# Experts' second product of one token group with the weights standing and 384 tokens moving

## The chip, the core and the metric

The kernel runs on one core of one Trainium2 chip. A core has TensorE (PE, matmuls), VectorE (DVE), ScalarE (ACT), GpSimd (POOL) and SyncE (SP, which here only issues DMAs), each with its own instruction queue, and 16 DMA engines that they share. The metric is the device time of one execution in microseconds; three runs of the kernel before gave a median of 1117.77 (1117.68 to 1119.88).

## The reference

Everything is float32. Attention without softmax, a bilinear layer, and a mixture of four experts follow one another:

```python
kv  = einsum('bhsd,bhse->bhde', k, v)            # 4 x 8 heads, 576 tokens, 64 wide
out = einsum('bhsd,bhde->bhse', q, kv)
x   = out / sqrt(mean(out**2) + 1e-6) * g_norm   # -> [2304 tokens, 512]
x   = ((x @ w1) * (x @ w2) @ w3) @ w_out         # 1024 wide inside
p   = domain_probs / (domain_probs.sum(-1) + 1e-9)
for e in range(4):                               # the experts
    y += p[:, e] * (relu(x @ e_w1[e]) @ e_w2[e]) # 512 -> 1024 -> 512
```

The change touches the experts' second product, `relu(...) @ e_w2[e]`, its scaling by the token's share `p[:, e]`, the sum over the experts, and the store of the result.

## The kernel before

A float32 value is held as two parts, high and low, and a product is three matmuls (high x high, low x high, high x low), by the helper `mm3` (L321 to L325); so nearly all of TensorE's time stands under L323 to L325. Larger products are cut in two each way and done by a seven-product scheme (Winograd's form of Strassen) in place of eight.

The 2304 tokens go through the experts in three groups of 2 x 384 tokens (`GROUPS`, `W = 384`; a part of a group is three tiles of 128 tokens). The first group computes the second product plainly (`down`) and spills the weights and their sums to DRAM (`w2_kept`). The second and the third group use `up` for the first product, with weight tiles of 128x128 standing and 384 tokens moving, and `down_product` (L1523) for the second. One call of `down_product` is one of the seven products of one expert (`PRODUCTS`, L1480): it loads the w2 operand in two DMAs of 512 KB into buffers of a pool of five (`RAWS`, L1531 to L1538), makes the token operand and splits it into high and low (`tokens_operand`, L1491, with sums at L1501 and splits at L368 and L373), and then, for each of the three token tiles, lets the tokens stand (128x128) and 256 columns of w2 move: 4 pieces x 3 passes (L1545 to L1550). The sums of the seven products collect in four PSUM banks, two (`at`) by two; a product that ends a target or feeds one is read out by `collect_half` (L1564), which multiplies by the share, a number per token and so per partition, and adds to the tile's accumulator in one VectorE operation (L1576); the first one of a tile is a ScalarE or VectorE operation that writes it (L1580, L1582). When the last expert has been added, `store_tile` (L1616) stores the 128 tokens x 512 on SyncE's queue in one DMA.

The order of all work is written by a planner (`Plan.order`, L139). Each operation has durations for the engines that may do it, a stage (its place in the list of items built at L1648 to L1677), and buffers. The planner runs a list schedule with these durations: an engine that is free takes the ready operation of the earliest stage, up to 14 stages ahead (`WINDOW`), if its buffers fit (99 SBUF tiles of 2 KB a partition, 8 PSUM banks), so matmuls of the second product fill the places where the first product waits for its bank. On the chip each engine then runs its list in that order, waiting on semaphores. VectorE's operations between SBUF tiles and GpSimd's are marked as sharing one port (`ported`, L116) and are not planned at the same time. The items of one expert's second product stand among those of the next expert's first product; at a change of group three products (`AHEAD`) stand before it. The shares `pn` are computed once in the front part (`expert_shares`, L1637).

Of the kernel before, what the change touches and what calls it, by code (L numbers as in the profile page):

```python
# [9 lines left out]
F32 = mybir.dt.float32  # L10
# [5 lines left out]
ALU = mybir.AluOpType  # L16
AX = mybir.AxisListType

P = 128
# [4 lines left out]
WINDOW = 14  # L24
AHEAD = 3
LATER = 6
PLAIN = 1
SUMMING = 18
WARM = 10
# [66 lines left out]
class Plan:  # L96
# [11 lines left out]
    def add(self, engines, emit, reads=(), writes=(), latency=0.2, stage=None, free=False, hold=None):  # L108

        op = Op(engines, emit, self.stage if stage is None else stage, latency)
        op.hold = hold
        op.ported = {e for e in engines if e == "pool" or (e == "dve" and not free)}  # L116
        op.pinned = stage is not None
        for accesses, write in ((reads, False), (writes, True)):
            for access in accesses:
                buf, key = access if isinstance(access, tuple) else (access, None)  # L120
                if buf not in op.bufs:
                    op.bufs.append(buf)
                    buf.users += 1
                for other, k, w in buf.touched:
                    if other is not op and (write or w) and (k is None or key is None or k == key):
                        op.deps.append(other)
                buf.touched.append((op, key, write))
        op.index = len(self.ops)
        self.ops.append(op)
        return op  # L130
# [128 lines left out]
def attention_moe_kernel(  # L259
# [26 lines left out]
    nc = tc.nc  # L286
    B, H, S, D = q.shape
    NT, DM = out.shape
    FF = moe_w1.shape[1]
    NE = e_w1.shape[0]  # L290
    HP = H // 2
    KD = DM // P
    KF = FF // P
    R = 4
    M = R * P
# [12 lines left out]
    plan = Plan({"r": RAWS, "h": TILES, "n": 4, "c": 2, "b": BANKS, "d": 1000, **RINGS})  # L308
    add = plan.add
# [4 lines left out]
    def bank():  # L314
        return Buf("b", "b", [P, 512], F32)

    def half(name, dt=F32, ring=None):
        return Buf("h", name, [P, 512], dt, ring)


    def mm3(ps, w, x, first, last, more=False):  # L321

        nc.tensor.matmul(ps, w[0], x[0], start=first, stop=False, skip_group_check=more)  # L323
        nc.tensor.matmul(ps, w[0], x[1], start=False, stop=False, skip_group_check=more)  # L324
        nc.tensor.matmul(ps, w[1], x[0], start=False, stop=last, skip_group_check=more)  # L325

    def t_act(n, psum=False):
        return (0.157 if psum else 0.19) + n / 1200

    def t_dve(n):  # L330
        return 0.143 + n / 960
# [4 lines left out]
    def t_pe(n, passes=3):  # L336
        return passes * (0.0137 + n / 2400)
# [16 lines left out]
    def spilled(name, buf, value=whole, later=0):  # L354

        d = Buf("d", name, [P, 512], F32, tag=name)
        add(
            {"sp": 0.73}, lambda _: nc.sync.dma_start(out=d[:, :], in_=value(buf.tile)),
            reads=[buf], writes=[d], latency=2.4, stage=plan.stage + later,
        )  # L360
        return d
# [41 lines left out]
    ident = const.tile([P, P], F32, name="ident")  # L403
    g8 = const.tile([P, 1], F32, name="g8")
    pn = const.tile([P, NT // P, NE], F32, name="pn")
# [4 lines left out]
    xscale, share = Buf("c", "xscale", None, None), Buf("c", "share", None, None)  # L410
# [258 lines left out]
    def evacuate(dst, src, n, to, value, key=None):  # L669
        add(  # L670
            {"act": t_act(n, True), "dve": t_dve(n)},
            lambda e: nc.scalar.copy(to(dst.tile), value(src.tile)) if e == "act"  # L672
            else nc.vector.tensor_copy(out=to(dst.tile), in_=value(src.tile)),
            reads=[src], writes=[(dst, key)], free=True,
        )
# [191 lines left out]
    def pair_weights(g, n, i):  # L867
# [3 lines left out]
        f0, f1 = i, i + KF // 2  # L871
        if g and i < PLAIN:
            raw = Buf("r", "wval", [P, 2, 512], F32)
# [12 lines left out]
        else:  # L886
            vals = [weight(n, f) for f in (f0, f1)]
            if i < PLAIN:
                w12_kept[n, i] = [
                    spilled(f"w{n}kept{i}_{j}", val, later=LATER) for j, val in enumerate(vals)  # L890
                ]
                made = pair_w[g, n, i] = {}, [Pair("w"), Pair("w")]
                for val, w in zip(vals, made[1]):
# [4 lines left out]
                [  # L898
                    spilled(f"w{n}_{i}_{m}_{part}", t, lambda t: t.bitcast(F32), later=LATER)
                    for part, t in enumerate(pair.parts)  # L900
# [6 lines left out]
    def weight(n, f):  # L907

        if (n, f) not in weights:
            weights[n, f] = decode(f"w{n + 1}", columns((moe_w1, moe_w2)[n], f), True)  # L910
        return weights[n, f]

    def bilinear_plain(b, i):

        ws = [pair_weights(0, n, i)[1] for n in range(2)]
        for j, f in enumerate((i, i + KF // 2)):
            multiplied(b, f, [w[j] for w in ws])
            ab[b, f] = spilled(f"ab{b}kept{f}", ab[b, f], later=LATER)

    def bilinear_pair(g, i):  # L920
# [77 lines left out]
        for b in (b0, b1):  # L998
            for f in (f0, f1):
                ab[b, f] = spilled(f"ab{b}kept{f}", ab[b, f], later=LATER)  # L1000

# [130 lines left out]
    W = 384  # L1132
    TILES3 = W // P
# [12 lines left out]
    def token_tile(g, i, t):  # L1146
        whole_block, half_block, at = GROUPS[g]
        return (whole_block, 2 * i + t) if t < 2 else (half_block, at // P + i)
# [342 lines left out]
    def tokens_operand(g, e, name, i):  # L1491

        a = {
            f"a{part + 1}{k + 1}": h32[g, e, i + k * KF // 2, part] for part in range(2) for k in range(2)
        }

        def sum_of(name, x, y, op):
            t = sums[g, e, name, i] = half(name)
            add(
                {"dve": t_dve(W)},  # L1500
                lambda eng: nc.vector.tensor_tensor(  # L1501
                    out=t[:, :W], in0=x[:, :W], in1=y[:, :W], op=op
                ),
                reads=[x, y], writes=[t],
            )
            return t

        def get(name):
            if name in a:
                return a[name]  # L1510
            if (g, e, name, i) in sums:
                return sums[g, e, name, i]
            x, y, op = {
                "s1": ("a21", "a22", ALU.add), "s2": ("s1", "a11", ALU.subtract),
                "s3": ("a11", "a21", ALU.subtract), "s4": ("a12", "s2", ALU.subtract),
            }[name]
            return sum_of(name, get(x), get(y), op)

        s = Pair("ht")
        split(s, get(name), W, lambda t: t[:, :W], lambda t: t[:, :W])  # L1520
        return s

    def down_product(g, e, n):  # L1523
        left, right, at, start, targets = PRODUCTS[n]
        if n == 0:
            yacc[g, e] = [[bank(), bank()] for _ in range(2)]
        banks = yacc[g, e][at]
        k = W2_OPERANDS.index(right)
        kept = w2_kept[e]
        lefts, rights = [], []  # L1530
        for i0 in range(0, KF // 2, 2):  # L1531
            raw = Buf("r", "w2", [P, 2, 2, 256], F32R)
            add(
                {"sp": 1.46},
                lambda _, raw=raw, i0=i0: nc.sync.dma_start(out=raw.tile.bitcast(F32), in_=kept.tile[:, k, i0:i0 + 2]),
                reads=[kept], writes=[raw], latency=2.4,
            )
            rights += [(raw, 0), (raw, 1)]  # L1538
        for i in range(KF // 2):
            lefts.append(tokens_operand(g, e, left, i))  # L1540
        for t in range(TILES3):
            ps = banks[t // 2]
            c = slice(t % 2 * 256, t % 2 * 256 + 256)

            def mms(_, t=t, ps=ps, c=c):  # L1545
                for i, (h, (raw, r)) in enumerate(zip(lefts, rights)):
                    mm3(
                        ps[:, c], h[:, t * P:(t + 1) * P], (raw[:, r, 0], raw[:, r, 1]),
                        start and i == 0 and t % 2 == 0, i == KF // 2 - 1, True,
                    )  # L1550


            op = add(
                {"pe": t_pe(256, 3 * KF // 2)}, mms,
                reads=[p for h in lefts for p in h.parts] + [raw for raw, _ in rights[::2]],
                writes=[(ps, t)],
            )
            if t % 2:
                op.deps.append(before)
            before = op  # L1560
            for part, half_ in targets:
                collect_half(g, e, part, t, half_, ps, c, n)
# [74 lines left out]
    def expert_shares():  # L1637
        add({"sp": 1.0}, load_probs, writes=[share], latency=3.0)
        add({"dve": 0.6}, shares, writes=[share])

    front = {
        fn.__name__: fn for fn in (
            bilinear_pair, bilinear_plain, expert_shares, mixed, mixed_product,
            norm_scale, rest_unit, row, unit, w3o_summed,
            w_out_tile, weight,
# [15 lines left out]
    for g in range(1, len(GROUPS)):  # L1661
        for e in range(NE):
# [4 lines left out]
            for i in range(KF // 2):  # L1667
                item(up, g, e, i)
                n = -(-len(waiting) // (KF // 2 - i))
# [56 lines left out]
```

## Time and profile before

| | |
|---|---|
| Median of three runs | 1117.77 us |
| The profiled execution | 1117.49 us |
| Its span, first to last instruction | 1115.7 us |
| Mean granted TensorE clock (share of full) | 0.998 |
| TensorE busy, share of the span | 99% |
| VectorE, ScalarE, GpSimd busy | 73%, 54%, 4% |
| Bytes moved by DMA | 272.91 MB, 245 GB/s on average |
| DMA queues | SyncE's 72.5% of 16 engines; none of GpSimd |

A row of the profile that groups instructions has the line of the kernel, the engine, the operation, what it writes and reads by the program's names, the shapes, the count, the busy time in us and the mean of one in ns, then the engine's idle time before them with what ended it. Matmuls are pipelined: the busy time of one overlaps the next, so their spacing is read from the starts in the timeline. The first token group of the experts ends about 660 us, the second about 900 us with its last products among the third group's first ones; from 1078 us to the end only second products of the last expert remain.

### The profile page before, as it was taken

The page shows a single profiled execution, that of the slowest core. Times are in us where ns is not written, and L with a number is a line of the kernel's source. Part 1 is how long each engine was busy: PE and PEld are TensorE (multiplying, and loading weights), DVE is VectorE, ACT ScalarE, POOL GpSimd, SP SyncE. Part 2 cuts the span into 40 slices and gives each one's busy share as a digit, 9 for nine tenths or more (in the row PEclk, how much of TensorE's full clock was granted, in tenths as well). Part 3 has the DMA queues.
Part 4 walks back from the last instruction along what each step waited for, and adds up shares of the span by engine and source line. Part 5 has one row for each costly group of instructions (what it writes and reads, how often), then busy time and mean ns, then how long its engine had stood idle before and what let it go on. Part 6 is the DMA issues. An engine that isn't in the chain of part 4 may idle for free.

```text
span 1115.7 us, 19375 instructions
## 1 busy us (share of the span) xinstructions
PE 1103.3 (99%) x6856; PEld 1022.3 (92%) x6856; DVE 810.5 (73%) x1656; ACT 600.6 (54%) x1472; POOL 47.1 (4%) x57
## 2 busy tenths in 40 slices
PE   7999999999999999999999999999999999999998
PEld 7888888888888999889999999999999999999998
DVE  4888888889879898788667745547588646474684
ACT  6998754556636655545444455434455445444540
POOL 4513200000000000000000000000000000000000
PEclk9999999999999999999999999999999999999999
DMA  9999993450330599999977935778679867685846
GB/s 272 288 336 329 380 370 102 137 167 20 95 95 29 171 349 351 345 365 327 339 262 239 363 126 198 259 247 288 217 256 328 282 239 259 238 299 195 280 140 203
DMA packets 173697, 272.91 MB, mean 245 GB/s; under 512 B 21792, under 2 KB 89376, under 8 KB 173600
## 3 DMA queue, kind: packets, MB, share of 16 engines
q1 hardware_dynamic: 173440, 271.68, 72.5%
q8 instruction: 54, 0.88, 0.3%
q14 instruction: 43, 0.35, 0.1%
q10 hardware_dynamic: 160, 0.00, 0.0%
HBM read 188.78 MB, written 82.84 MB: 243 GB/s over the span
## 4 chain that ended last, share of the span: by engine, by line
PE 95%; ACT 2%; DMA 1%; DVE 1%; issue 0%; POOL 0%; DVEq 0%; ACTq 0%
PE b L323 30%; PE b L325 30%; PE b L324 30%; PE b L684 2%; PE b L741 1%; PE b L713 1%; DMA q<-in_q_dram 0%; ACT x L592 0%; ACT hth L368 0%; DMA w1raw<-in_moe_w_dram 0%; DMA woraw<-in_moe_w_out_dram 0%; PE b L776 0%; DVE s L1501 0%; DVE acc L1576 0%; ACT qs L729 0%
## 5 line engine op out<-in xcount | busy, mean ns | idle before, releaser
L672 ACT COPY u<-b 128x384 f32<-128x384 f32 (+1 forms) x191 | 96.5, 505 | 194.5 <-PE b L325 189.7
L325 PE MATMUL b<-w,htl 128*128 128x256 f32 x672 | 189.9, 283 | 0.0
L324 PE MATMUL b<-w,hth 128*128 128x256 f32 x672 | 189.8, 282 | 0.0
L323 PE MATMUL b<-w,hth 128*128 128x256 f32 x672 | 189.6, 282 | 0.0
L1401 DVE TENSOR_TENSOR u<-u,b 128x384 f32<-128x384 f32 x144 | 79.5, 552 | 124.2 <-PE b L325 66.9
L1576 DVE SCALAR_TENSOR_TENSOR acc<-b,pn,acc 128x256 f32<-128x256 f32 x144 | 68.7, 481 | 85.1 <-PE b L325 84.9
L325 PEld LDWEIGHTS b<-w,htl 128*128 128x128 f32 x672 | 128.4, 191 | 0.0
L323 PEld LDWEIGHTS b<-w,hth 128*128 128x128 f32 x672 | 128.0, 191 | 0.2
L324 PEld LDWEIGHTS b<-w,hth 128*128 128x128 f32 x672 | 128.1, 191 | 0.0
L368 ACT CAST hth<-s 128x384 fp32r<-128x384 f32 x128 | 62.9, 512 | 51.1 <-DVE s L1501 48.0
L1412 ACT ACTIVATE u<-u 128x384 f32<-128x384 f32 x96 | 50.5, 526 | 62.0 <-DVE u L1401 61.9
L325 PE MATMUL b<-wdh,htl 128*128 128x512 f32 x192 | 75.5, 393 | 0.0
L324 PE MATMUL b<-wdl,hth 128*128 128x512 f32 x192 | 75.4, 393 | 0.0
L323 PE MATMUL b<-wdh,hth 128*128 128x512 f32 x192 | 74.7, 389 | 0.0
L373 DVE TENSOR_TENSOR htl<-s,hth 128x384 fp32r<-128x384 f32 x128 | 67.3, 550 | 3.5 <-ACT hth L368 3.5
L373 DVE TENSOR_TENSOR htl<-u,hth 128x384 fp32r<-128x384 f32 x96 | 49.9, 551 | 5.8 <-ACT hth L368 5.8
L368 ACT CAST hth<-u 128x384 fp32r<-128x384 f32 x96 | 46.3, 510 | 0.4
L323 PE MATMUL b<-th,weh 128*128 128x512 f32 x112 | 44.5, 397 | 0.4 <-ACT u L672 0.4
L325 PE MATMUL b<-th,wel 128*128 128x512 f32 x112 | 43.7, 390 | 0.0
L324 PE MATMUL b<-tl,weh 128*128 128x512 f32 x112 | 43.7, 390 | 0.0
L325 PEld LDWEIGHTS b<-wdh,htl 128*128 128x128 f32 x192 | 36.0, 188 | 7.6
L324 PEld LDWEIGHTS b<-wdl,hth 128*128 128x128 f32 x192 | 36.0, 188 | 5.9
(291 smaller groups left out, 3037.8 us busy)
## 6 DMA issues: line engine op xcount, KB each, us to landing
we<-we SPq DMA_DIRECT2D x240, 256.0 KB, 5.3
w<-w2kept SPq DMA_DIRECT2D x112, 512.0 KB, 4.5
we<-weh SPq DMA_DIRECT2D x48, 256.0 KB, 3.8
we<-wel SPq DMA_DIRECT2D x48, 256.0 KB, 3.7
w3raw<-in_moe_w_dram SPq DMA_DIRECT2D x16, 512.0 KB, 3.7
e1raw<-in_moe_w_dram SPq DMA_DIRECT2D x32, 256.0 KB, 4.4
e2raw<-in_moe_w_dram SPq DMA_DIRECT2D x32, 256.0 KB, 4.4
w2kept<-wth SPq DMA_DIRECT2D x32, 256.0 KB, 3.8
```

Of the source, the lines that this page charges most:

```text
L323: nc.tensor.matmul(ps, w[0], x[0], start=first, stop=False, skip_group_check=more)
L324: nc.tensor.matmul(ps, w[0], x[1], start=False, stop=False, skip_group_check=more)
L325: nc.tensor.matmul(ps, w[1], x[0], start=False, stop=last, skip_group_check=more)
L368: nc.scalar.copy(to(dst.high.tile), value(src.tile))
L373: nc.vector.tensor_tensor(out=to(dst.low.tile), in0=value(src.tile), in1=to(dst.high.tile), op=ALU.subtract)
L672: lambda e: nc.scalar.copy(to(dst.tile), value(src.tile)) if e == "act"
L684: nc.tensor.transpose(ps[:, c], raw[:, c], ident)
L713: nc.tensor.matmul(ps[c, c], a, b_, start=r == 0, stop=r == R)
L741: nc.tensor.matmul(po[:, c], qt[:, c], kvb[b][:, p * P:(p + 1) * P], start=True, stop=True)
L1401: lambda _: nc.vector.tensor_tensor(out=t[:, :W], in0=base[:, :W], in1=ps[:, :W], op=ALU.add),
L1412: lambda eng: nc.scalar.activation(out=t[:, :W], in_=src[:, :W], func=ACTF.Relu)
L1576: nc.vector.scalar_tensor_tensor(out=a[:, to], in0=ps[:, c], scalar=sc, in1=a[:, to], op0=ALU.mult, op1=ALU.add)
```

## The change

In the second group (`TURNED = (1,)`) `down_product` lets w2 stand and the tokens move: for each half `j` of the 256 output columns, 128 columns of w2 stand and 384 tokens move, 4 pieces x 3 passes into one bank. The result has output columns on the partitions and tokens along the row, so a token's share is no longer a number per partition. In the front part the shares are transposed on TensorE and stored to DRAM (`turned_shares`); for each expert and part, three DMAs on SyncE's queue load one row of them each, spread to all 128 partitions (`spread_shares`). `collect_wide` copies the unfinished targets out of their bank, adds the last product to them, multiplies by the spread shares and adds the experts. After the last expert each of the eight results (2 parts x 4 blocks of 128 columns) is transposed in 32x32 blocks on VectorE, and stored by GpSimd's queue: per token tile and block of 32 columns one DMA of 32 partitions x 4 x 32 numbers, 96 DMAs in all, which the planner places from six stages later on, four to a stage. GpSimd operations marked `free` no longer count as sharing the port; only the new stores are.

```diff
+TURNED = (1,)
-        op.ported = {e for e in engines if e == "pool" or (e == "dve" and not free)}
+        op.ported = {e for e in engines if e in ("pool", "dve") and not free}
...
+    def turned_shares():
+        ps, rows = bank(), half("rows")
+        n = NT // P * NE
+        add({"pe": 0.11}, lambda _: nc.tensor.transpose(ps[0:n, 0:P], pn.rearrange("p t e -> p (t e)"), ident), ...)
+        add({"act": t_act(P, True), "dve": t_dve(P)}, ... rows[0:n, 0:P] <- ps[0:n, 0:P] ..., free=True)
+        add({"sp": 0.3}, lambda _: nc.sync.dma_start(out=shares_kept[:, :], in_=rows[0:n, 0:P]), ..., latency=2.4)
...
+    def spread_shares(g, e, part):
+        if (g, e, part) not in spread:
+            t = spread[g, e, part] = half("spread")
...
+            def emit(_):
+                for m, row_at in enumerate(places):
+                    nc.sync.dma_start(
+                        out=t[:, m * P:(m + 1) * P],
+                        in_=shares_kept[row_at:row_at + 1, :].to_broadcast([P, P]),
+                    )
+            add({"sp": 0.9}, emit, reads=[shares_kept], writes=[t], latency=2.6)
+        return spread[g, e, part]
...
+    def collect_wide(g, e, part, column, j, ps, n):
+        at = column * 2 + j
...
+        last = {(0, 0): 1, (0, 1): 5, (1, 1): 4, (1, 0): 6}[part, column]
+        key = g, e, part, at
+        if n != last:
+            firsts[key] = half("y")
+            evacuate(firsts[key], ps, W, w, w)
+            return
+        scale = spread_shares(g, e, part)
+        if (part, column) == (1, 0):
+            y = half("y")
+            both(y, ps, scale, ALU.mult, True, [ps, scale])
+        else:
+            y = firsts.pop(key)
+            both(y, y, ps, ALU.add, True, [ps])
+            both(y, y, scale, ALU.mult, False, [scale])
+        if e == 0:
+            wide[g, part, at] = y
+            return
+        acc = wide[g, part, at]
+        both(acc, acc, y, ALU.add, False, [y])
+        if e == NE - 1:
+            store_wide(g, part, at, acc)
+
+    def store_wide(g, part, at, acc):
+        t = half("o")
+        add({"dve": t_dve(W)}, lambda _: nc.vector.transpose(out=t[:, :W], in_=acc[:, :W]), reads=[acc], writes=[t])
+        for m in range(TILES3):
+            b, tile_at = token_tile(g, part, m)
+            rows = out[b * S:b * S + M, :].rearrange("(k p r) n -> p k r n", r=R, p=32)[:, :, tile_at]
+            for a in range(4):
+                def store(_, rows=rows, a=a, m=m):
+                    c = slice(at * P + a * 32, at * P + a * 32 + 32)
+                    src = t[a * 32:(a + 1) * 32, m * P:(m + 1) * P]
+                    nc.gpsimd.dma_start(out=rows[:, :, c], in_=src.rearrange("p (k d) -> p k d", d=32))
+                add({"pool": 1.2}, store, reads=[t], stage=plan.stage + 6 + len(wide_stored) // 4, free=True)
+                wide_stored.append(t)
...
     def down_product(g, e, n):
...
+        if g in TURNED:
+            for j, ps in enumerate(banks):
+                def wide_mms(_, j=j, ps=ps):
+                    c = slice(j * P, (j + 1) * P)
+                    for i, (h, (raw, r)) in enumerate(zip(lefts, rights)):
+                        mm3(
+                            ps[:, :W], (raw[:, r, 0, c], raw[:, r, 1, c]), h[:, :W],
+                            start and i == 0, i == KF // 2 - 1, True,
+                        )
+                add({"pe": t_pe(W, 3 * KF // 2)}, wide_mms, ..., writes=[ps])
+                for part, column in targets:
+                    collect_wide(g, e, part, column, j, ps, n)
+            return
...
     def expert_shares():
...
+        turned_shares()
```

## Rows read from the trace of the kernel before

**Rows 1.** The page: busy time by engine; the chain that ended last, by engine.
```profile
PE 1103.3 (99%) x6856; PEld 1022.3 (92%) x6856; DVE 810.5 (73%) x1656; ACT 600.6 (54%) x1472; POOL 47.1 (4%) x57
...
PE 95%; ACT 2%; DMA 1%; DVE 1%; issue 0%; POOL 0%; DVEq 0%; ACTq 0%
```

**Rows 2.** TensorE's waits, 667 to 1116 us: total us, times, longest.
```profile
PE b L323 <- ACT u L672: 1.0, 4, 0.3
```

**Rows 3.** Timeline of TensorE about 697 us: start, us, what.
```profile
697.04 0.34 PE L325 MATMUL b<-x21h,we 128*128 128x384 f32 x1
...
697.59 0.44 PE L323 MATMUL b<-t2h,we 128*128 128x384 f32 x1 [0.20 <-ACT u L672]
```

**Rows 4.** Busy time by stretch: us, each engine's (instructions), clock, DMA share, GB/s.
```profile
660.00:850.00 190.00, 189.56 (x1346) 188.76 (x1345) 116.27 (x252) 92.37 (x211) 0.00 (x0) 1.00 0.69 235
850.00:1116.00 266.00, 260.69 (x1869) 259.43 (x1867) 162.88 (x346) 113.23 (x244) 0.00 (x0) 1.00 0.71 244
```

**Rows 5.** Timeline of TensorE: first matmuls of runs of one shape; the last matmul.
```profile
700.82 0.28 PE L323 MATMUL b<-w,hth 128*128 128x256 f32 x1
...
702.25 0.34 PE L323 MATMUL b<-x22h,we 128*128 128x384 f32 x1
...
704.33 0.28 PE L323 MATMUL b<-w,hth 128*128 128x256 f32 x1
...
711.52 0.34 PE L323 MATMUL b<-x11h,we 128*128 128x384 f32 x1
...
715.68 0.28 PE L323 MATMUL b<-w,hth 128*128 128x256 f32 x1
...
1110.95 0.28 PE L325 MATMUL b<-w,htl 128*128 128x256 f32 x1
```

**Rows 6.** TensorE's transposes (min/median/max ns); GpSimd's longest group.
```profile
L684 PE MATMUL b<-ident,val x64: 270/273/273, 246.0 to 291.1; 128*128 128x128 f32 x64
...
L605 POOL TENSOR_TENSOR ss<-ss,power 128x8 f32<-128x8 f32 x18 | 31.7, 1761 | 1.5
```

**Rows 7.** VectorE's and ScalarE's groups by shape, 667 to 860 us.
```profile
L1576 DVE SCALAR_TENSOR_TENSOR acc<-b,pn,acc 128x256 f32<-128x256 f32 x60 | 28.7, 481 | 32.8 <-PE b L325 32.7
L1401 DVE TENSOR_TENSOR u<-u,b 128x384 f32<-128x384 f32 x36 | 19.9, 552 | 34.4 <-ACT u L672 17.2 <-PE b L325 16.6 <-ACT hth L368 0.7
...
L672 ACT COPY u<-b 128x384 f32<-128x384 f32 x37 | 17.7, 477 | 44.0 <-PE b L325 42.6 <-issue 1.2
L1580 ACT ACTIVATE acc<-b,pn 128x256 f32<-128x256 f32 x12 | 5.7, 472 | 7.6 <-PE b L325 7.6
```

**Rows 8.** Waits of SyncE's queue, 667 to 1116 us.
```profile
SPq L1535 <- PE b L325: 186.2, 65, 23.7
...
SPq L1620 <- DVE acc L1576: 20.0, 8, 4.7
SPq L345 <- PE b L325: 16.1, 21, 3.7
```

**Rows 9.** Stores of the result and weight loads: issue (min/median/max ns), landing.
```profile
L1620 SPq DMA_DIRECT2D out_dram<-acc x16: 337/338/422, 641.3 to 1110.8; - x16
...
DMA to landing us min/median/max: 2.1/2.5/4.9
...
we<-we SPq DMA_DIRECT2D x240, 256.0 KB, 5.3
```

**Rows 10.** VectorE's groups by shape, 850 to 1116 us, costliest first.
```profile
L1576 DVE SCALAR_TENSOR_TENSOR acc<-b,pn,acc 128x256 f32<-128x256 f32 x90 | 42.9, 481 | 53.9 <-PE b L325 53.8
...
L373 DVE TENSOR_TENSOR x22l<-xf,x22h 128x128 fp32r<-128x128 f32 x2 | 0.6, 286 | 0.0
```

**Rows 11.** SyncE's DMA queue, 0 to 25 and 850 to 1110 us: packets, MB, share.
```profile
q1 hardware_dynamic: 8357, 6.61, 100.1%
...
q1 hardware_dynamic: 25856, 63.83, 71.2%
```

**Rows 12.** Busy time by stretch, where the third group begins.
```profile
850.00:875.00 25.00, 24.97 (x176) 24.66 (x175) 22.68 (x51) 10.39 (x22) 0.00 (x0) 1.00 1.02 374
```

More of the change, by code (lines that the diff above doesn't have):

```diff
@@ L1521, in tokens_operand @@
         return s
+    shares_kept = Buf("d", "shares", [NT // P * NE, P], F32, tag="shares")
+    def turned_shares():
+        ps, rows = bank(), half("rows")
+        n = NT // P * NE
+        add(
+            {"pe": 0.11}, lambda _: nc.tensor.transpose(ps[0:n, 0:P], pn.rearrange("p t e -> p (t e)"), ident),
+            reads=[share], writes=[ps],
+        )
+        add(
+            {"act": t_act(P, True), "dve": t_dve(P)},
+            lambda e: nc.scalar.copy(rows[0:n, 0:P], ps[0:n, 0:P]) if e == "act"
+            else nc.vector.tensor_copy(out=rows[0:n, 0:P], in_=ps[0:n, 0:P]),
+            reads=[ps], writes=[rows], free=True,
+        )
+        add(
+            {"sp": 0.3}, lambda _: nc.sync.dma_start(out=shares_kept[:, :], in_=rows[0:n, 0:P]),
+            reads=[rows], writes=[shares_kept], latency=2.4,
+        )
@@ new lines, in attention_moe_kernel @@
+    spread = {}
+    def spread_shares(g, e, part):
+        if (g, e, part) not in spread:
+            t = spread[g, e, part] = half("spread")
+            places = []
+            for m in range(TILES3):
+                b, tile_at = token_tile(g, part, m)
+                places.append((b * R + tile_at) * NE + e)
+            def emit(_):
[3 more added lines that the diff above has]
+                        in_=shares_kept[row_at:row_at + 1, :].to_broadcast([P, P]),
+                    )
+            add({"sp": 0.9}, emit, reads=[shares_kept], writes=[t], latency=2.6)
+        return spread[g, e, part]
@@ new lines, in attention_moe_kernel, with w, both @@
+    wide_stored = []
+    firsts = {}
+    wide = {}
+    def collect_wide(g, e, part, column, j, ps, n):
+        at = column * 2 + j
+        def w(t):
+            return t[:, :W]
+        def both(out, a, b, op, free=False, reads=()):
+            add(
+                {"dve": t_dve(W)},
+                lambda _: nc.vector.tensor_tensor(out=w(out), in0=w(a), in1=w(b), op=op),
+                reads=reads, writes=[out], free=free,
+            )
+        last = {(0, 0): 1, (0, 1): 5, (1, 1): 4, (1, 0): 6}[part, column]
[19 more added lines that the diff above has]
+            store_wide(g, part, at, acc)
@@ new lines, in store_wide @@
+    def store_wide(g, part, at, acc):
+        t = half("o")
+        add(
+            {"dve": t_dve(W)}, lambda _: nc.vector.transpose(out=t[:, :W], in_=acc[:, :W]),
+            reads=[acc], writes=[t],
+        )
+        for m in range(TILES3):
+            b, tile_at = token_tile(g, part, m)
+            rows = out[b * S:b * S + M, :].rearrange("(k p r) n -> p k r n", r=R, p=32)[:, :, tile_at]
[6 more added lines that the diff above has]
+                wide_stored.append(t)
@@ L1540, in down_product @@
             lefts.append(tokens_operand(g, e, left, i))
+        if g in TURNED:
[6 more added lines that the diff above has]
+                            start and i == 0, i == KF // 2 - 1, True,
+                        )
+                add(
+                    {"pe": t_pe(W, 3 * KF // 2)}, wide_mms,
+                    reads=[p for h in lefts for p in h.parts] + [raw for raw, _ in rights[::2]],
+                    writes=[ps],
+                )
+                for part, column in targets:
+                    collect_wide(g, e, part, column, j, ps, n)
+            return
         for t in range(TILES3):
```

## The prediction, made before the changed kernel was seen

> **What bounds the kernel now.** I read the page's busy time first: TensorE is busy 99% of the span, VectorE 73%, ScalarE 54%, GpSimd 4% [rows 1]. A busy TensorE can hide waits, so the chain of waits comes second: 95% of the chain that ended last is TensorE [rows 1]. Third, the list of waits: over the second and third group TensorE waited only 1.0 us for a named releaser, four times, at most 0.3 us [rows 2]; where it stood still, as at 697.04, the step to the next matmul is 0.55 us instead of 0.17 [rows 3]. I counted five such steps between 660 us and the end, 0.36 to 0.62 us each, some 1.8 us beyond the usual step. So the time of these stages is the number of matmuls times their spacing, and only a change in that product, or a new wait, moves the end. VectorE is busy 116.3 of 190 us in the second group's stretch and 162.9 of 266 in the third's, the DMA engines about 70% in both [rows 4]: both have room, on average.
>
> **The change, part by part.** *Matmuls.* A product of the second group has 3 token tiles x 4 pieces x 3 passes = 36 matmuls of 256 columns; afterwards it has 2 output halves x 4 x 3 = 24 of 384. The columns are the same (9216). There are 28 products (7 for each of 4 experts): 1008 matmuls become 672. The busy time of a matmul (282 ns) overlaps its neighbour, so I take start-to-start times. From 704.33 to 711.52 us lie 60 matmuls of 256 columns: 7.19/60 = 119.8 ns. From 711.52 to 715.68 lie 24 of 384: 4.16/24 = 173.3 ns [rows 5]. Those 384 are the first product's, with the same shape (weights of 128x128 standing, 384 moving) that the second product gets, so the new form has a price of this trace. A short run of 12 goes from 700.82 to 702.25: 119.2 ns [rows 5]. Before: 1008 x 0.1198 = 120.8 us, or 120.2 by the short run. After: 672 x 0.1733 = 116.5. The gain is 3.7 to 4.3 us; I take 4.0. All of it is on the path.
>
> Here a page speaks against the change. By rows, 128 more columns cost 53.5 ns, 0.418 ns each, which leaves 12.8 ns per matmul that columns don't explain; 336 matmuls fewer, at 12.8 ns, is the same 4.3 us [rows 5]. The Trainium skill ("TensorE: Matmul & The Clock Gate", section "Wait — 56ns, not 53.3ns?") gives a fixed cost of about 2.5 ns per matmul beyond its columns; by that the gain would be 336 x 2.5 ns = 0.8 us. This trace has five times that in both shapes, so the measurement decides.
>
> *Transposed shares.* One 72-row transpose on TensorE, its copy and a small store are added in the front part. The nearest row, a transpose by the same identity, is 273 ns busy [rows 6]; the lower end is one spacing, 0.12. I take 0.1 us, range 0.1 to 0.3. The copy and the store lie beside TensorE's work.
>
> *Collecting.* Removed: 84 collects of 256 columns, of which 12 (the first ones) run on ScalarE at 472 ns and 72 on VectorE at 481 ns, 34.6 us [rows 7]. Added per expert: 8 last steps out of PSUM and 6 multiplications by the shares, and for three experts 8 additions more, so 14 + 3 x 22 = 80 operations of 384 columns at 552 ns, 44.2 us, and 8 transposes. No row shows a VectorE transpose; between one operation of its size, 0.55 us, and four of them, one per block of 32 rows [rows 7], lie 4 to 18 us, and I take the lower, 4.4. VectorE gets 14 us more over some 190, 61% becoming about 69%. ScalarE gets 24 copies of 0.48 us, 11.4, for the 5.7 removed. Both lie beside TensorE; without that cover the price is a wait per bank, like the 0.4 us of the step in rows 3. A bank is next written two products later, and a product lasts 4.2 us, so the chain add, multiply, add (1.7 us) fits.
>
> *SyncE's queue.* Added: 24 broadcast loads of 64 KB, 0.34 us issue each by the row of a tile store [rows 9]; removed: the second group's six tile stores, for which the queue stood waiting on VectorE (all eight such waits with the third group's: 20.0 us). The queue stands 186 us waiting for TensorE's last pass to give back w2 buffers, and for tile buffers only 16 us [rows 8]; it is ahead. What is queued behind a broadcast load that comes late is VectorE's multiplication and all its later work; it is needed twice per expert, and a DMA lands in 2.1 to 5.3 us [rows 9]. Tile buffers: 8 accumulators instead of 6, up to 4 waiting copies and 2 share tiles more. I take 0, range 0 to 4 us of TensorE's waiting.
>
> *GpSimd's stores.* 8 results x 3 token tiles x 4 partition blocks = 96 DMAs, each of 128 pieces of 128 bytes, 12288 in all. GpSimd has nothing else to do then [rows 4], and the trace has no DMA issued by it. An issue lies between SyncE's 0.34 us and GpSimd's longest operation, 1.76 us for 8 columns [rows 6, 9]; I take 1.2, nearer to GpSimd's own row: 115 us, hidden. The first can start when the second product of the last expert is collected, about 850 us, and the matmuls end at 1111.2 us [rows 5], so they are hidden up to 261/96 = 2.7 us each. Nothing on another engine waits for them but the reuse of eight tiles.
>
> A page speaks against this too. In the third group's stretch VectorE does only operations with two tensor inputs (eleven groups, of which the first and the last stand here) [rows 10]. By the Trainium skill ("SBUF — State Buffer", section "SBUF: two separate sides") a copy between tiles on VectorE locks GpSimd out of writing its descriptors, and a transfer of 620 ns took 3100. By 3.1 us the queue would last 298 us, past the end. The same page ("Who interferes with whom") exempts operations with two tensor inputs, so no run here shows the lock, and I expect none.
>
> *The DMA engines.* At the start 8357 packets of 0.8 KB filled the 16 engines for about 22 us, 42 ns each; in the third group 25856 packets of 2.5 KB took 71.2% of 260 us, 115 ns each [rows 11]. The line through both gives about 9 ns for 128 bytes. So 12288 pieces cost 12288 x 9/16 = 7 us to 12288 x 42/16 = 32 us of all engines, spread over 115 us or more: 6% to 28% beside 71%. I take the lower end for most of the range and no wait for TensorE.
>
> **Sum.** Profiled execution 1117.49 us (span 1115.7 and 1.8 around it): - 4.0 + 0.1 = 1113.6. The median is 0.28 above that execution, so 1113.9 us.
>
> **Rivals.** (a) *The waits eat it.* The planner lists everything anew; with blocks of 2.1 us (12 matmuls of 384) in place of 1.4 to fill a wait, and more tiles held, four to eight more steps like rows 3, 0.4 to 0.5 us each, cost 2 to 4 us: 1116 to 1118. For it: its five steps now. Against it: two fillers per weight block suffice now, and 14 blocks for 4 weight blocks still give them.
> (b) *Slower: the stores crowd out weights.* In 850 to 875 us the DMA engines are full (1.02) and GpSimd may issue 32 of its stores at once. At 42 ns these 4096 pieces take 10.8 us of the engines; weights arrive later by that, and TensorE waits: 1113.9 + up to 10.8 = 1125. It decides from the point where a piece costs over about 25 ns, since SyncE's lead (a product and a half, 6 us) hides 4096 x 25/16 = 6.4 us. For it: the full engines [rows 12]. Against it: the line through the packets.
> (c) *Slower: the store queue lasts past the end*, above 2.7 us each; at 3.0 it would be 1113.9 + 96 x 0.3 = 1143.
> (d) *Columns alone count*: the 12.8 ns don't go because another limit sets the spacing; then 1117.8 (by the page's rule above 1117.0). Against it: rows 5.
> (e) *The new order also drops the five standing steps*: 1112.
>
> **How the numbers follow.** Forecast (1112.5 to 1115.4) 0.57, (a) 0.20, (b) 0.09, (c) 0.03, (d) 0.03, (e) 0.08. A measurement of this kernel tells about 0.2%, 2.2 us, from no change: below 1115.5 is faster, above 1120.0 slower. Faster holds the forecast and (e), less a little: 0.63; same holds (a) and (d) and that little: 0.25; slower (b) and (c): 0.12. The range leaves out (c), most of (b) and a little below (e): 1112.0 to 1119.5; the forecast alone 1112.5 to 1115.4.
>
> **What would show it.** Right: in the second group 672 matmuls of 384 columns by w2 in place of 1008 of 256, 173 ns apart, the third group some 4 us earlier and as long as before, TensorE's waits under 2 us, GpSimd done well ahead of the last matmul. Wrong: new TensorE waits on w or we loads between 850 and 900 us (b), GpSimd's last store as the end of the chain (c), steps of 120 ns per 256 columns kept (d), steps of 0.5 us at block ends (a).

## The result, and the profile after

The changed kernel takes 1127.27 us (median of six runs, 1125.37 to 1128.07) against 1117.16 us for the kernel before (six runs, 1116.14 to 1119.88): ratio 1.0086, 95% interval 1.0072 to 1.0100. By this ratio, which is one of means, it is 9.6 us slower, by the medians 10.1; 1113.9 was forecast. The profiled execution took 1127.08 us, with a span of 1125.2 and a mean granted clock of 0.995. Line numbers are one higher up to L1520 and over a hundred higher behind: the matmuls are now L324 to L326. The results' transposes are L1608 and their stores L1620.

The page after, busy time and the chain that ended last by engine and by line, answers to [rows 1]:

```profile
PE 1101.2 (98%) x6521; PEld 1020.5 (91%) x6521; DVE 825.0 (73%) x1672; ACT 605.7 (54%) x1485; POOL 100.1 (9%) x153
...
PE 90%; POOL 3%; DMA 3%; issue 1%; DVE 1%; ACT 1%; SPq 0%; ACTq 0%; DVEq 0%; POOLq 0%
```

TensorE has 335 instructions fewer (336 matmuls less, one transpose more) and is busy only 2 us less; its share of the chain fell from 95% to 90%, and GpSimd, which stood at 0%, is in the chain with 3%. Something of GpSimd's now lies on the way to the end. Next, the waits of TensorE from 667 us to the end (us in total, times, longest), which answer to [rows 2]:

```profile
PE b L324 <- ACT u L673: 12.8, 4, 7.0
PE b L324 <- DVE u L1402: 0.6, 1, 0.6
```

The same releaser as before, a ScalarE copy out of a PSUM bank, but 12.8 us in place of 1.0. The windows say where (the stretch and its length in us, then the busy time and instructions of TensorE, its weight loads, VectorE, ScalarE and GpSimd, then the granted clock, the DMA share and GB/s); the first line answers to [rows 4], the third to [rows 12]:

```profile
660.00:850.00 190.00, 189.43 (x1093) 189.11 (x1092) 127.02 (x263) 97.26 (x220) 3.01 (x6) 1.00 0.74 253
825.00:850.00 25.00, 25.00 (x146) 25.00 (x145) 23.06 (x52) 15.98 (x40) 3.01 (x6) 1.00 0.96 326
850.00:875.00 25.00, 17.99 (x103) 17.67 (x102) 12.04 (x28) 9.09 (x21) 10.38 (x19) 0.92 0.86 303
875.00:900.00 25.00, 25.00 (x139) 25.00 (x138) 19.00 (x39) 11.48 (x24) 14.27 (x26) 0.94 0.75 258
900.00:925.00 25.00, 20.11 (x127) 19.79 (x126) 9.71 (x20) 9.67 (x21) 21.46 (x40) 0.93 0.43 125
925.00:950.00 25.00, 24.36 (x171) 24.04 (x170) 16.59 (x35) 13.71 (x32) 3.85 (x7) 1.00 0.77 267
```

Up to 850 TensorE is as full as before (189.4 of 190 us; 189.6 [rows 4]), so the second group has lost nothing up to there. TensorE loses 7 us in the stretch 850 to 875 and 5 us in 900 to 925, and VectorE and ScalarE have *less* to do there than next door: they wait too. For whom, the timeline of VectorE, of ScalarE, and of GpSimd at that place shows (start, us, instruction, idle before and its releaser; the last line, start, us and what, is from the chain that ended last):

```profile
861.02 0.56 DVE L374 TENSOR_TENSOR htl<-s,hth 128x384 fp32r<-128x384 f32 x1 [0.58 <-ACT hth L369]
872.35 1.03 DVE L1502 TENSOR_TENSOR s<-u,s 128x384 f32<-128x384 f32 x2 [10.76 <-DMA out_dram<-o]
...
872.94 0.98 ACT L369 CAST hth<-s 128x384 fp32r<-128x384 f32 x2 [9.87 <-DVE s L1502]
873.82 0.47 ACT L673 COPY u<-b 128x384 f32<-128x384 f32 x1
...
846.99 4.03 POOL L1620 DMA_DIRECT2D out_dram<-o  x7 [714.68 <-DVE o L1608]
852.57 0.56 POOL L1620 DMA_DIRECT2D out_dram<-o  x1 [1.56 <-issue]
...
862.59 4.55 POOL L1620 DMA_DIRECT2D out_dram<-o  x8 [1.11 <-issue]
...
866.58 5.64 DMA out_dram<-o
```

And TensorE beside it:

```profile
867.00 0.34 PE L326 MATMUL b<-hth,w 128*128 128x384 f32 x1
874.35 0.69 PE L324 MATMUL b<-t1h,we 128*128 128x384 f32 x1 [7.01 <-ACT u L673]
874.83 0.52 PE L325 MATMUL b<-t1l,we 128*128 128x384 f32 x1
875.15 0.52 PE L326 MATMUL b<-t1h,we 128*128 128x384 f32 x1
...
878.10 0.34 PE L324 MATMUL b<-hth,w 128*128 128x384 f32 x1
...
907.07 0.34 PE L326 MATMUL b<-t3h,we 128*128 128x384 f32 x1
912.30 0.69 PE L324 MATMUL b<-t2h,we 128*128 128x384 f32 x1 [4.89 <-ACT u L673]
```

Read backwards, that is one chain. TensorE stands from 867 to 874.35 because a bank has not been copied out (L673). ScalarE would copy it, but two casts of `s` (L369) stand ahead in its list, and they wait for VectorE to make `s` (L1502). This `s` is no work of the next group: it is `s4`, a token operand of the sixth of the seven products of the second group's last expert. The first two results are finished after two of these products, so their tiles come round while the same expert still runs; the second group's matmuls by w2 run until 901.9 us. VectorE waits 10.76 us for a DMA out of a result tile `o`, because `s` was given the memory of the second result's tile. In the compiled program that instruction waits for three completions on each of eight semaphores: the first 24 stores, those of the first two results. The 24th was issued at 866.6 and landed at 872.2. The profile gives the whole list of the results' stores, first the stores (durations in ns, first and last start) and who waited for them (us, times):

```profile
L1620 POOL DMA_DIRECT2D out_dram<-o x96: 548/548/769, 847.0 to 928.9; - x96
...
  DVE s L1502: 10.8, 1
  ACT hth L369: 6.8, 1
  DVE htl L374: 5.3, 1
...
DMA to landing us min/median/max: 1.7/4.1/7.5
```

and SyncE's queue, where a weight load was held up in the same way:

```profile
SPq L346 <- DMA out_dram<-o: 7.7, 1, 7.7
```

The wait of 6.8 us (ScalarE's `hth`, an operand of the third group, up to 910.9) is behind the second pause, 907.07 to 912.30; that of 5.3 us cost TensorE under 1 us.

**What paces the stores.** An issue takes 0.55 us, so 24 of them could be done in 13.2 us; from 847.0 to the last start at 866.6 they took 19.6, with gaps of 6.5 us in all. The trace records when each store landed. Of the 22 gaps over 0.1 us in GpSimd's stores, 21 end 0.31 us after the store *seventh* before has landed, and the other one waits for a transpose: the first store landed at 852.26 and the eighth was issued at 852.57. Never were more than seven under way. In the seven kernels here that store from GpSimd's queue, 162 of 171 such gaps end so. So behind the first seven the landings pace the stores too, and with them the time at which a tile comes free. With no such gaps and the same landing the 24th store would have landed some 6.5 us sooner; by this estimate they make up over half of VectorE's wait.

**Balance.** From the first group's last 512-column matmul to the last matmul of all, before:

```profile
648.54 0.40 PE L325 MATMUL b<-wdh,htl 128*128 128x512 f32 x1
```

and after:

```profile
646.65 0.40 PE L326 MATMUL b<-wdh,htl 128*128 128x512 f32 x1
...
1120.39 0.28 PE L326 MATMUL b<-w,htl 128*128 128x256 f32 x1
```

Before, 1110.95 [rows 5] - 648.54 = 462.4 us; after, 1120.39 - 646.65 = 473.7: 11.3 us more. (This profiled run came to the mark 1.9 us sooner, so the spans differ by 9.5 only. The profiled runs of the kernels below come to it between 646.80 and 649.49, the one without the change of the second product at 648.28; so that is no effect of the change.) The pauses account for it: 867.00 to 874.35 is 7.2 us over the usual step of 0.17. The twelve steps behind it, to 878.10, ten of them slow, took 3.75 us in place of 12 x 0.173 = 2.08, thus 1.7 more. The second pause is 5.1 us, and its slow steps cost 1.5. Together 15.4 us lost, and some 4 gained.

### The profile page after: what moved, and what is told of

It is laid out like the page before. It is cut to its first block, busy times and chain, and to the rows that moved or that the text cites. A ratio compares the mean times of both kernels' runs of the same rounds, so it can differ in the third digit from the quotient of the medians.

```text
span 1125.2 us, 18942 instructions
## 1 busy us (share of the span) xinstructions
PE 1101.2 (98%) x6521; PEld 1020.5 (91%) x6521; DVE 825.0 (73%) x1672; ACT 605.7 (54%) x1485; POOL 100.1 (9%) x153
## 3 DMA queue, kind: packets, MB, share of 16 engines
q0 software_dynamic: 3072, 1.58, 0.6%
## 4 chain that ended last, share of the span: by engine, by line
PE 90%; POOL 3%; DMA 3%; issue 1%; DVE 1%; ACT 1%; SPq 0%; ACTq 0%; DVEq 0%; POOLq 0%
PE b L324 29%; PE b L325 29%; PE b L326 29%; POOL out_dram L1620 3%; PE b L685 2%; DMA out_dram<-o 1%; PE b L742 1%; DMA kv<-in_v_dram 1%; DMA q<-in_q_dram 1%; PE b L714 1%; DMA graw<-in_g_norm_dram 1%; SPq L346 0%; DMA woraw<-in_moe_w_out_dram 0%; PE b L777 0%; ACT u L673 0%
## 5 line engine op out<-in xcount | busy, mean ns | idle before, releaser
L673 ACT COPY u<-b 128x384 f32<-128x384 f32 (+1 forms) x191 | 96.4, 505 | 187.7 <-PE b L326 183.3
L1620 POOL DMA_DIRECT2D out_dram<-o x96 | 53.0, 552 | 744.1 <-DVE o L1608 727.5
L324 PE MATMUL b<-w,hth 128*128 128x256 f32 x336 | 95.1, 283 | 0.0
L326 PE MATMUL b<-w,htl 128*128 128x256 f32 x336 | 95.1, 283 | 0.0
L325 PE MATMUL b<-w,hth 128*128 128x256 f32 x336 | 95.1, 283 | 0.0
L369 ACT CAST hth<-s 128x384 fp32r<-128x384 f32 x128 | 63.2, 513 | 53.8 <-DVE s L1502 42.7
L326 PE MATMUL b<-wdh,htl 128*128 128x512 f32 x192 | 75.5, 393 | 0.0
L324 PE MATMUL b<-hth,w 128*128 128x384 f32 x224 | 75.2, 336 | 0.0
L325 PE MATMUL b<-htl,w 128*128 128x384 f32 x224 | 75.1, 335 | 0.0
L326 PE MATMUL b<-hth,w 128*128 128x384 f32 x224 | 75.0, 335 | 0.0
L324 PE MATMUL b<-wdh,hth 128*128 128x512 f32 x192 | 74.7, 389 | 0.0
L1697 DVE SCALAR_TENSOR_TENSOR acc<-b,pn,acc 128x256 f32<-128x256 f32 x72 | 34.2, 481 | 41.7 <-PE b L326 41.4
L325 PEld LDWEIGHTS b<-w,hth 128*128 128x128 f32 x336 | 64.4, 192 | 0.0
L326 PEld LDWEIGHTS b<-w,htl 128*128 128x128 f32 x336 | 64.4, 192 | 0.0
L324 PEld LDWEIGHTS b<-w,hth 128*128 128x128 f32 x336 | 64.4, 192 | 0.0
L369 ACT CAST hth<-u 128x384 fp32r<-128x384 f32 x96 | 46.4, 511 | 0.4
L324 PE MATMUL b<-th,weh 128*128 128x512 f32 x112 | 44.5, 397 | 0.3 <-ACT u L673 0.3
```

What stands on the lines that cost most here:

```text
L369: nc.scalar.copy(to(dst.high.tile), value(src.tile))
L1620: nc.gpsimd.dma_start(out=rows[:, :, c], in_=src.rearrange("p (k d) -> p k d", d=32))
L1697: nc.vector.scalar_tensor_tensor(out=a[:, to], in0=ps[:, c], scalar=sc, in1=a[:, to], op0=ALU.mult, op1=ALU.add)
```

## The experiments

Theory R: other work, of the second or the third group, is given a result's tile and waits until GpSimd's stores have landed. (The text written before the first run speaks of the third group alone.) Rival C: the many small pieces fill the DMA engines, so that weights come late. Rival N: the new order by itself leaves TensorE waiting, with or without stores. Ratios are to the kernel before, with 95% intervals. Edits are against the changed kernel, with omitted lines marked by `...`. "The mark" is the last 512-column matmul, as above.

### Results in tiles of their own

```diff
-TILES = 99
+TILES = 93
...
+        "o": ctx.enter_context(tc.tile_pool(name="op", bufs=8)),
...
-        t = half("o")
+        t = Buf("o", "o", [P, W], F32)
```

> The eight transposed results get tiles of their own (8 of 1.5 KB a partition) which nothing else uses; the shared tiles go from 99 to 93 to make room. Theory R (work of the third group is placed in tiles whose stores have not landed, and waits for them): the waits of VectorE and ScalarE for the result's DMAs at 861 to 872 and 904 to 911 us vanish, and the 4 us of the matmuls remain: 1113.5 to 1115 us. Theory C (the 12288 small pieces slow the weight loads): the stores are the same, so 1125 or more. Theory N (the new order of the list): anywhere, but TensorE waits outside 850 to 935 us.

Measured: 1117.52 us, ratio 0.9997 (0.9988 to 1.0007). No engine but GpSimd waits for the results' DMAs, which land as late as in the changed kernel (1.7 to 6.4 us, median 4.5), and TensorE's pauses behind 850 us are gone. But the time is 2.5 us above the 1113.5 to 1115 that R expected. Six tiles fewer for everything else cost: steps of TensorE over the usual one add up to 5.6 us between 390 us and the end, all of them ahead of 850 us, where the kernel before has 2.6 in all. That is 3.0 us; the profiled execution (1115.48) is near the lowest of the twelve (1115.34 to 1119.63), and why their median lies 2 us above it stays open. Same stores, same pieces, no pause: this speaks for R and against C.

### Six tiles fewer, results in shared tiles

```diff
-TILES = 99
+TILES = 93
```

> The changed kernel with 93 shared tiles in place of 99 and the results still in shared tiles: the price of the six tiles alone. R: the reuse of the results' tiles stays, and with fewer tiles it comes sooner: 1125 to 1135 us. C: about 1127, as with 99.

Measured: 1135.48 us, ratio 1.0167 (1.0151 to 1.0183), just above the 1125 to 1135 of R. The waits of VectorE and of SyncE for the results' DMAs:

```profile
DVE s L1502 <- DMA out_dram<-o: 10.0, 1, 10.0
DVE htl L374 <- DMA out_dram<-o: 6.5, 1, 6.5
DVE o L1608 <- DMA out_dram<-o: 0.9, 1, 0.9
...
SPq L346 <- DMA out_dram<-o: 31.6, 8, 9.4
```

With equally many shared tiles, the run with the results' own tiles is 18 us faster. So it was not the smaller number of tiles that helped there; by itself it does harm. TensorE's steps over the usual one add up to 6.4 us between 390 and 850 us (5.6 with the results' own tiles, 0.9 in the changed kernel), and behind 850 to 17.1 (0 and 17.1): the price of six tiles and the price of the results' stores stand apart.

### No stores

All stores of the results but the first of the 96 are left out.

```diff
-                add({"pool": 1.2}, store, reads=[t], stage=plan.stage + 6 + len(wide_stored) // 4, free=True)
+                if not wide_stored:
+                    add({"pool": 1.2}, store, reads=[t], stage=plan.stage + 6, free=True)
```

> Only the first of the 96 stores of the second group is made; the other 95 are left out, so that part of the output is not written. R and C both: no waits for the result's DMAs, 1113 to 1114.5 us. N: stays above 1117.

Measured: 1112.97 us, ratio 0.9956 (0.9943 to 0.9969). TensorE's waits from 667 us on are 0.8 us in two. The stretch from the mark to the last matmul is 1106.09 - 648.68 = 457.4 us, 5.0 less than before. That is what everything in the change but the stores gives back: the forecast's 4.0 and a little more. So the stores cost 14 us, and N falls.

### Twice the pieces

Own tiles as in the first experiment, and each store made a second time, into memory that nobody reads:

```diff
+    again = pools["d"].tile([32, 2, 4, TILES3, 4, 4, 64], F32, tag="again", name="again")
...
+                    nc.gpsimd.dma_start(out=again[:, part, at, m, a, :, 0:32], in_=src.rearrange("p (k d) -> p k d", d=32))
```

> As the kernel with eight tiles of the results' own, with every store made twice, the second time into a scratch buffer in DRAM: 24576 small pieces. It measures what the pieces cost where no tile is reused. R: the same as with single stores, 1116 to 1118.5 us. C: the waits for weights come with twice the pieces: 1122 or more.

Measured: 1115.58 us, ratio 0.9984 (0.9975 to 0.9994), just under the 1116 to 1118.5 of R and not slower than with single stores (0.9997). GpSimd's queue in the profile of the changed kernel (packets, MB, share of 16 engines):

```profile
q0 software_dynamic: 3072, 1.58, 0.6%
```

and in this one:

```profile
q0 software_dynamic: 6144, 3.16, 1.1%
```

The amount doubled, and TensorE is full from 850 to 950 us, beside DMA engines 70 to 97% busy. The rate rose less, since the 192 issues go from 852.9 to 991.5 us in place of 847.0 to 928.9 (again seven under way at the most); but at the rate of the changed kernel the first experiment has no pause either. C falls. Why this kernel came out 2 us below the one with single stores was not looked into.

### The rest of the change alone

```diff
-TURNED = (1,)
+TURNED = ()
```

The second product is the old one; the shares are still transposed and stored in the front part.

> TURNED = (): every group with the tokens standing as before, but the shares are still transposed and stored in the front part. It has the small additions in front and a newly listed order, without the change to the second product. R and C: 1117 to 1117.8 us, as before. N: a time away from before by more than 2 us.

Measured: 1117.62 us, ratio 0.9998 (0.9990 to 1.0007). The transposed shares cost nothing that can be measured.

### The planner told that the tile is free later

```diff
-                add({"pool": 1.2}, store, reads=[t], stage=...)
+                add({"pool": 1.2}, store, reads=[t], latency=8.0, stage=...)
```

> The changed kernel with one number altered: the planner is told that a store lands 8 us after its issue, so it counts a result's tile as held until then. R, if the planner's count decides which tile is reused when: the waits go, 1113 to 1116 us. R, if the tile that is handed out is chosen elsewhere, in the order in which the program is written: waits stay, 1120 to 1128. C: 1125 or more.

Measured: 1128.46 us, ratio 1.0091 (1.0077 to 1.0105): nothing gained. VectorE waits 10.3 and 9.2 us for the results' stores, ScalarE 3.6. By the first form of R the fault is the planner's short count of a store (it calls the tile free just after the issue), and the waits would go; they stayed, so that form fell. The planner counts how many tiles are free, not which; which tile an operation gets is settled when its list is compiled, and there `s` still got the one of the second result.

### The same stores from SyncE's queue

```diff
-                    nc.gpsimd.dma_start(out=rows[:, :, c], ...)
+                    nc.sync.dma_start(out=rows[:, :, c], ...)
...
-                add({"pool": 1.2}, store, ...)
+                add({"sp": 0.6}, store, ..., latency=2.4, ...)
```

> The same 96 stores from the same shared tiles, on SyncE's queue instead of GpSimd's, planned at 0.6 us each with 2.4 us to land. R: a result's tile is free about as soon as its last store lands, and the issues (0.35 to 0.55 us each, 35 to 53 us in all) stand ahead of weight loads in that queue: 1114 to 1122 us. C: the pieces are the same, 1125 or more.

Measured: 1113.90 us, ratio 0.9963 (0.9950 to 0.9977). The results are in shared tiles, and nobody waits for them:

```profile
L1620 SPq DMA_DIRECT2D out_dram<-o x96: 315/422/1457, 855.2 to 1020.7; - x96
...
DMA to landing us min/median/max: 1.5/4.4/7.2
```

The time is just under the 1114 to 1122 that R expected. One DMA lands as late as from GpSimd's queue. But SyncE issues them among its loads, spread over 165 us in place of 82, and the planner lists them where they fit among these. So a shared tile isn't a fault by itself either; it costs when the tile comes round to an operation on the path before its last store has landed.

### Two tiles of their own, stores listed at once

```diff
+        "o": ctx.enter_context(tc.tile_pool(name="op", bufs=2)),
...
-        t = half("o")
+        t = Buf("o", "o", [P, W], F32)
...
-                add({"pool": 1.2}, store, reads=[t], stage=plan.stage + 6 + len(wide_stored) // 4, free=True)
+                add({"pool": 0.75}, store, reads=[t], latency=6.0, stage=plan.stage, free=True)
```

> Two tiles for the results alone (3 KB a partition, which fit beside the 99 shared ones), stores issued at their own stage instead of six and more later, and the planner told 0.75 us for an issue and 6 us until it has landed. R: nothing else waits for the stores, and no shared tile is lost, so it gets near the kernel without stores (1112.97): 1112.5 to 1114.5 us. C: the small pieces are all still there and closer together: 1117 or more.

Measured: 1112.30 us, ratio 0.9952 (0.9938 to 0.9965), faster than both kernels and level with the one without stores. The windows of the place where the changed kernel stood still:

```profile
850.00:875.00 25.00, 25.00 (x146) 25.00 (x146) 19.79 (x44) 13.25 (x30) 13.93 (x27) 1.00 1.02 373
875.00:900.00 25.00, 25.00 (x147) 25.00 (x146) 17.46 (x35) 12.64 (x28) 18.59 (x34) 1.00 0.76 254
900.00:925.00 25.00, 25.00 (x184) 25.00 (x183) 12.24 (x26) 12.47 (x28) 17.60 (x32) 1.00 0.63 194
```

TensorE is full, although the DMA engines are as full as before the change (1.02 [rows 12]) and GpSimd issues some 25 stores in the first of them (13.93 us at 0.55).

### Stores listed at once, in shared tiles

The last version changed two things. This one has the second alone (the last two lines of its diff).

> The best version so far changed two things at once: two tiles that only results use, and stores that the planner lists in the stage of their transpose, with 0.75 us for an issue and 6.0 us until the tile is free. This run does the second alone: the results stay in the 99 shared tiles. Theory R (other work gets a result's tile and waits for its stores): own tiles are what helped, so waits of VectorE, ScalarE or SyncE for the results' stores are there again, at least 5 us in all, with steps of TensorE of several us between 850 and 930 us, and the time is 1117 to 1128 us. Rival (issuing the stores sooner is enough): no engine but GpSimd waits for the results' stores, and the time is 1111 to 1114 us, as with the own tiles.

Measured: 1122.79 us, ratio 1.0050 (1.0038 to 1.0062). Who waited for the results' DMAs, by the list of their line (us, times):

```profile
  ACT hth L369: 9.1, 3
  ACT u L673: 5.7, 1
  DVE htl L374: 5.3, 1
```

and in SyncE's queue:

```profile
SPq L346 <- DMA out_dram<-o: 22.4, 8, 10.9
```

TensorE has one pause of 7.0 us (at 916.39) and half-speed steps behind it. By the ratios, issuing sooner gives 4.0 us of the 15 back (1.0086 to 1.0050); the other 10.9 come from the two tiles (to 0.9952). R holds.

## Why the prediction was wrong

**Matmuls: right.** The new form runs as the rows said. Two neighbouring runs of the second product after:

```profile
699.93 0.33 PE L324 MATMUL b<-hth,w 128*128 128x384 f32 x1
...
702.01 0.33 PE L324 MATMUL b<-x22h,we 128*128 128x384 f32 x1
```

Twelve in 2.08 us is 173.3 ns each, the figure taken from [rows 5]; all 672 are in the trace, between 665.6 and 901.9 us. Without stores the stretch is 5.0 us shorter: 3.7 to 4.3 of it is the forecast's gain by rows, and 0.8 are long steps that went (2.4 to 1.6 us in sum behind the mark). That is part of (e); (d) would have given nothing. The Trainium skill ("TensorE: Matmul & The Clock Gate", section "Wait — 56ns, not 53.3ns?") has a fixed cost of about 2.5 ns per matmul, by which the gain would be an estimated 0.8 us; the measurement doesn't agree.

**VectorE and ScalarE: right.** VectorE 825.0 against 810.5 us, 14.5 more for 14 forecast; ScalarE 5.1 more for 5.7. A transpose takes 0.57 us, the lower end taken (0.55). Up to 850 us TensorE has one step over 0.3 us in the second group's stretch, 0.90 us at 797.5, where it had two of 0.55 and 0.58; so the wait chains of the collecting fit, as argued. The broadcast loads came in time (VectorE waited 0.4 us for one).

**GpSimd's issue: sized too high, and harmless.** 0.55 us each and not 1.2, so 53 us and not 115; with the gaps, 82 us from first to last. No issue took over 0.77 us, and the last one starts at 928.9. So (c) was out of reach, and nothing is seen of the lock of GpSimd's descriptors that the prediction weighed: the gaps follow the landings of earlier stores. The first starts at 847.0 (about 850 forecast).

**Pieces: the count and the line were wrong, the price right by luck.** The line through the prediction's own two points (42 ns at 0.8 KB, 115 ns at 2.5 KB) gives 13 ns for 128 bytes, not 9, and so 10 us of all engines, not 7. A store of 128 pieces of 128 bytes shows as 32 packets of 0.5 KB, 3072 in all, at 35 ns each. They take 0.6% of the engines' time, 0.006 x 1125 = 7 us, which is the lower end of the forecast's 7 to 32. (b) fell with the doubled stores.

**The failed step** is the sentence "Nothing on another engine waits for them but the reuse of eight tiles", whose exception got no price and no rival. The reuse was seen and not followed up: who gets the tile, when, and what stands behind it. The result's tiles are of the 99 that all work shares, so the next users are operands and weights of the second group's last products and of the third group, on VectorE, ScalarE and SyncE. Twelve stores read one tile, and it is free only when the last one has landed: 12 x 0.55 us of issue at the least, gaps until the seventh store before has landed, and up to 7.5 us of landing. For these stores the forecast has a figure for the issue alone. What the runs showed in its place is waits of 10.8 and 5.3 us on VectorE, 6.8 on ScalarE and 7.7 on SyncE's queue, and 14 us for the stores in all. The queues are in order: VectorE's wait of 10.8 us held ScalarE's casts, these held the copy out of the bank, and that held TensorE. The same reasoning was applied in the prediction to the broadcast loads on SyncE's queue, and not to the stores.

**What a pause costs** was also not counted: after both pauses TensorE ran for 2 to 3 us at half speed, 1.7 and 1.5 us more. The chance given to "slower" went to (b) and (c), the mishaps of the DMA engines and of the queue; a wait by memory was the third that was missing. (a) had the right victim (TensorE at block ends), but at 0.4 to 0.5 us each.

That the tile is handed out when the list is compiled, and not by the planner's count, rests on one run and on the compiled program. Why just that `s` follows the second result there was not pursued.

## What to carry to other kernels

Where a new store reads a tile from a shared pool, price it as the last of its DMAs: issue of all of them, one after the other (slower, where the queue holds an issue back until an earlier store has landed), plus the latest landing. Then ask which operation is next in line for that tile and what is queued behind it. If this can be on the path, give the few tiles that wait for DMAs a pool of their own, as small as will do: two were enough here, and eight, taken from the rest, gave the gain away. Two experiments separate waiting for a tile from the load on the DMA engines: leave the stores out, and double them out of tiles of their own.

## What the runs showed of the hardware

- An issue of a strided store (32 partitions x 4 x 128 bytes) takes GpSimd 548 ns (at most 769), SyncE 422 ns (315 to 1457).
- From issue to landing it is 1.7 to 7.5 us, median 4.1, on GpSimd's queue and 1.5 to 7.2, median 4.4, on SyncE's; tile stores of the kernel before took 2.1 to 4.9 [rows 9].
- GpSimd's queue never had more than seven of these stores under way. It issues seven without a gap; in the changed kernel 21 of 22 gaps over 0.1 us, 0.14 to 1.9 us long, end 0.31 us after the landing of the seventh store before. The profile calls most of these gaps "issue", with no releaser. The compiled program has a store wait for the eighth before it at the nearest, so the limit of seven does not stand there; whether it goes by the number of stores or by their pieces was not tried.
- 3072 packets more on GpSimd's queue, beside DMA engines that are 70 to 97% busy, cost no time that can be measured.
- Behind both pauses (7.35 and 5.23 us from start to start) TensorE's clock was at its lower level, 1.2 GHz: the granted clock in the first pause, behind it, and then, and the same for the second pause (the stretch and its length in us, TensorE busy, clock, DMA share, GB/s):

```profile
867.30:874.30 7.00, 0.04 (x1) 0.76 1.03 365
874.35:877.60 3.25, 3.25 (x10) 0.50 0.64 238
878.20:890.00 11.80, 11.80 (x70) 1.00 0.82 285
907.40:912.20 4.80, 0.01 (x1) 0.97 0.23 62
912.30:914.30 2.00, 2.00 (x6) 0.50 0.19 32
```

A 384-column matmul then took a step of 0.32 us in place of 0.173.
